# Attention and a top-1 MoE on one core: a new order of the first steps, the roots of two units apart, the gains in two DMAs

## The chip, the core and the metric

The kernel runs on one core of one Trainium2 chip. The metric is the device time of one execution in microseconds. It is taken three times for the kernel before and shown with its median.

## What is computed

Per batch and head, 448 rows of q and k of 64 numbers are normed by their root mean square and multiplied by gains; then comes softmax attention, and a mixture of eight experts follows of which each token takes one.

```
rmsnorm(x, g) = x / sqrt(mean(x*x, -1) + 1e-6) * g
scores = rmsnorm(q, g_q) @ rmsnorm(k, g_k).T / 8        # 8 batches, 12 heads, 448 x 448
attn = exp(scores - max(scores)); attn /= sum(attn) + 1e-9
x = (attn @ v) as 3584 tokens x 768
e = argmax(x @ w_gate + modality_bias[modality_id]); p = softmax of the same at e
out = p * (relu(x @ w1[e]) @ w2[e])                     # 8 experts, 768 -> 1024 -> 768
```

## The kernel before

Attention is cut into 48 units of two heads. A unit takes seven steps of the main loop, one for each 128 of its 896 rows of scores; step n = 7u + j belongs to unit u. Steps from -22 to -1 are a prologue in which only the first units are prepared. The expert part runs behind and beside it; none of it changes here.

Instructions are issued in an order written out by hand, and each engine works through its own list in that order. The table `PLAN` says in which step a piece of a unit is issued. For unit u the pieces are:

- `ld`, the loads of q and k (L833, issued by SP); `lv`, those of v (L826).
- `sq` and `sk`, squares of q and of k. ACT writes them into one buffer for q and one for k (`sq_b`), and a reduction to one sum per row and head follows: one instruction on DVE, or a tree of six on POOL, in place in that buffer, for the pairs (unit, 0 for q or 1 for k) that `ps` lists. The next square of that side has to wait for the reduction.
- `rs`, the roots: two instructions on ACT (Ln, Exp, L53) and five small ones on POOL. Units go in groups of three; `rs0` says from which unit of its group the roots of an entry reach, so that one entry can cover one, two or three units.
- `nq` and `nk`, the norms (x times its root), on POOL; that of q of unit 0 is on DVE.
- `tk` and `tq`, the transposes (`tr{u}_{g}`, g = 0 for q, 1 for k; L908 on PE). ACT then takes the high part out of them and casts it to the places where the scores want it; for k it multiplies by `gs`, the product of both gains. DVE takes the low part, and SP moves some of it (L921).
- `sa`, scores for the row maxima (`sa{u}_{j}`, L985 and L990), each followed by a maximum on DVE.
- `mt`, the transpose of the maxima (L1001). ACT copies it out (7x128), and a DMA lays it into row 64 of the tile `ql` (L1006). That DMA is issued by ACT for the first two and the last three units, by SP for the others.
- `st`, the scores themselves (L1018), two halves: the second one takes the low part and the row of maxima. ACT takes the exponential of each (`st{u}_{j}`), and `av` (L1056, L1060) multiplies by v.
- `warm`, `warm1` and `warm2`: matmuls without use (L1341) that keep PE busy in the prologue. One such call shows as two matmuls in the trace.

`gain_product` makes `gs` on DVE from the gains that `load_gains` fetches. A step's lists are run in a fixed order: PE's work of the step, then what stood over for ACT and DVE, then the exponential, then the maxima, then casts that may wait; squares that a step issues have their reduction at the start of the next step's DVE list.

Of the kernel before, what the change touches and what calls it, by code (L numbers as in the profile page):

```python
# [66 lines left out]
def kernel(  # L67
# [739 lines left out]
    if True:  # L807
# [548 lines left out]
        def at(where, n, fn):  # L1356
            where.setdefault(n, []).append(fn)
# [66 lines left out]
        for n in range(P["start"], NJ * NU):  # L1424
# [22 lines left out]
                sums(*a)  # L1447
            for a in todo.get("gates", ()):
                at(pre["A"], n + 1, gates(*a))
            for a in todo.get("tr", ()):  # L1450
                a0, a1, a2, d_ = tr(*a)
                if a[0] < P["early"]:
                    at(pre["A"], n + 1, a1)
                    at(pre["A"], n + 1, a2)
                    at(pre["A"], n + P["late0"], a0)
                    at(pre["V"], n + P["late0"], d_)
                    continue
                at(pre["A"], n + 1, a0)
# [283 lines left out]
```

## Time and profile before

| | |
|---|---|
| time, median of 3 (lowest to highest) | 1041.18 us (1040.47 to 1041.79) |
| time of the profiled execution | 1043.32 us |
| its span, from the first to the last instruction | 1041.5 us |
| PE, ACT, DVE, POOL busy | 98%, 68%, 71%, 69% |
| mean granted clock of TensorE | 0.996 |

Times in rows are microseconds from the start of the span. Busy shares are means over a prologue in which PE mostly does warm-up work, 48 units of attention, and the experts behind them, so they say little about a stage.

### The profile page before, as it was taken

What the parts mean: (1) busy time and instruction counts of PE and PEld (TensorE: products, weight loads), DVE (VectorE), ACT (ScalarE), POOL (GpSimd) and SP (SyncE); (2) the same over time, 40 slices, a digit from 0 to 9 for tenths busy, and PEclk for the clock granted to TensorE, in tenths of its full rate; (3) what the DMA queues carried; (4) which work ended last, traced back from release to release, by engine and by line L of the source; (5) the groups of instructions that cost most, each with busy time, mean ns of one, the idle gap of its engine ahead of it and who ended that gap; (6) DMA issues with size and microseconds to landing.
All of it is one profiled execution on the core that took longest, in us unless ns stands there. A gap on an engine that the chain in (4) does not pass through costs nothing.

```text
span 1041.5 us, 18863 instructions
## 1 busy us (share of the span) xinstructions
PE 1017.7 (98%) x6462; PEld 820.2 (79%) x6462; DVE 742.2 (71%) x1260; ACT 710.0 (68%) x1379; POOL 718.2 (69%) x747
## 2 busy tenths in 40 slices
PE   8999999999999999999999999999999999999996
PEld 7655666666666666656659999999999999999995
DVE  5777888887888778886667987755675567656740
ACT  6897999889999889887655555645554455545531
POOL 6788798989788887888956646765645555565451
PEclk9999999999999999999999999999999999999998
DMA  6775658868677677665748506234572343234261
GB/s 181 193 172 131 160 139 191 166 143 183 157 170 160 156 177 156 163 119 119 230 120 285 92 17 188 71 92 122 162 263 74 110 122 92 62 92 123 74 201 63
DMA packets 147960, 148.20 MB, mean 142 GB/s; under 512 B 72762, under 2 KB 137742, under 8 KB 147344
## 3 DMA queue, kind: packets, MB, share of 16 engines
q1 hardware_dynamic: 122458, 105.08, 42.7%
q0 software_dynamic: 25328, 41.82, 12.8%
q8 instruction: 53, 0.87, 0.4%
q14 instruction: 51, 0.42, 0.2%
q10 hardware_dynamic: 70, 0.02, 0.0%
HBM read 150.31 MB, written 33.39 MB: 176 GB/s over the span
## 4 chain that ended last, share of the span: by engine, by line
PE 85%; DMA 4%; DVE 3%; ACT 3%; issue 2%; POOL 1%; SPq 1%; ACTq 0%; POOLq 0%; DVEq 0%
PE ph L608 23%; PE py L638 22%; PE st L1018 12%; PE av L1060 10%; PE sa L990 5%; PE av L1056 3%; PE tr L908 3%; PE xt L1126 2%; PE sm L1082 2%; DVE at_hlw L52 1%; PE sm L1089 1%; DMA w1w<-xw 1%; PE mt L1001 1%; DMA xrw<-xg 1%; DMA r<-in_q_dram 1%
## 5 line engine op out<-in xcount | busy, mean ns | idle before, releaser
L608 PE MATMUL ph<-xw,w1w 128*128 128x256 f32 x2016 | 246.3, 283 | 2.1 <-ACT at_w2lw L52 1.3
L608 PEld LDWEIGHTS ph<-xw,w1w 128*128 128x128 f32 x2016 | 243.9, 192 | 3.9 <-ACT at_w2lw L52 1.4
L52 DVE TENSOR_REDUCE at_hlw<-sa 128x1 f32<-128x448 f32 x336 | 205.0, 619 | 30.3 <-PE sa L985 15.2
L1018 PE MATMUL st<-w1w 128*128 128x448 f32 (+1 forms) x480 | 183.4, 431 | 1.5 <-ACT r2w L52 0.9
L52 POOL DMA_INDIRECT r<-in_moe_w_dram,tb_w x60 | 84.6, 1411 | 54.9 <-DVE w1w L52 39.7
L52 ACT ACTIVATE hhw<-ph 128x512 fp32r<-128x512 f32 x56 | 33.5, 598 | 123.4 <-PE ph L608 94.3
L52 ACT ACTIVATE r2w<-st 128x448 f32<-128x448 f32 x168 | 91.1, 545 | 34.6 <-PE st L1018 23.2
L638 PE MATMUL py<-w2lw,hhw 128*128 128x384 f32 x448 | 113.7, 334 | 0.0
L52 DVE TENSOR_TENSOR w1w<-r,w1w 128x768 fp32r<-128x768 f32 x112 | 104.9, 968 | 11.0 <-ACT w1w L52 9.8
L990 PE MATMUL sa<-w1w 128*128 128x448 f32 (+1 forms) x288 | 108.1, 376 | 3.0 <-DVE at_hlw L52 1.2
L52 ACT CAST w1w<-xw 64x448 fp32r<-64x448 f32 x188 | 105.9, 563 | 3.7 <-issue 1.4
L52 POOL DMA_INDIRECT r2w<-in_moe_w_dram,tb_vi x48 | 51.5, 1074 | 81.7 <-DVE w2lw L52 68.1
L52 DVE TENSOR_TENSOR w2lw<-r2w,w2ha 128x1536 fp32r<-128x1536 f32 x28 | 49.1, 1757 | 80.0 <-ACT w2ha L52 49.2
L1018 PEld LDWEIGHTS st<-w1w 128*128 128x128 f32 (+1 forms) x480 | 86.0, 190 | 24.6 <-issue 10.9
L1018 PE MATMUL st<-w1w,w2ha 65*128 65x448 f32 x288 | 100.6, 370 | 0.5 <-DMA w1w<-xw 0.5
L52 ACT ACTIVATE at_w2lw<-st 128x448 f32<-128x448 f32 x168 | 90.6, 545 | 12.5 <-PE st L1018 5.7
L52 POOL TENSOR_TENSOR xrw<-r,at_hlw 112x512 f32<-112x512 f32 x95 | 97.8, 1050 | 0.5
L52 POOL TENSOR_TENSOR r2w<-r2w 128x448 f32<-128x448 f32 (+1 forms) x72 | 83.3, 1157 | 21.3 <-DVE r2w L52 15.0
L52 ACT CAST w1w<-r 128x768 fp32r<-128x768 f32 x112 | 95.2, 903 | 0.1
L52 ACT ACTIVATE yw<-py,ltn 128x384 f32<-128x384 f32 x55 | 29.4, 579 | 77.0 <-PE py L638 48.5
L638 PEld LDWEIGHTS py<-w2lw,hhw 128*128 128x128 f32 x448 | 80.9, 188 | 0.0
L52 POOL TENSOR_TENSOR r2w<-r2w,at_w2lw 64x448 f32<-64x448 f32 (+1 forms) x48 | 55.3, 1151 | 32.8 <-DVE r2w L52 17.4
(302 smaller groups left out, 2210.2 us busy)
## 6 DMA issues: line engine op xcount, KB each, us to landing
w1w<-xw SPq DMA_DIRECT2D x216, 112.0 KB
xg<-xrw SPq DMA_DIRECT2D x14, 768.0 KB
xrw<-xg SPq DMA_DIRECT2D x56, 192.0 KB
r<-in_q_dram SPq DMA_DIRECT2D x19, 448.0 KB
r<-in_k_dram SPq DMA_DIRECT2D x19, 448.0 KB
w2ha<-xw SPq DMA_DIRECT2D x72, 112.0 KB
w1w<-w1w SPq DMA_DIRECT2D x48, 112.0 KB
r2w<-in_v_dram SPq DMA_DIRECT2D x24, 224.0 KB
```

What stands on the lines that cost most here:

```text
L52: return fn(*a, **kw)
L608: PE.matmul(ps[:, i], lhsT=lt_, rhs=rt_[:, c], start=n == 0, stop=n == 17)
L638: PE.matmul(ps[n][:, :384], lhsT=lt_[:, j, 128 * t : 128 * t + 128], rhs=rt_[:, 384 * n : 384 * n + 384], start=j == 0 and m == 0, stop=j ...
L908: PE.transpose(sp[:, c], src[:, c], idn[:CP, :CP])
L990: PE.matmul(ps[:, :S], lhsT=t["qq"][r, h, a : a + 128], rhs=t["kk"][h][r], start=True, stop=True)
L1001: PE.transpose(ps[0:NJ, :128], t["mx"], idn)
L1018: PE.matmul(ps[:, :S], lhsT=l, rhs=t["qq"][:, h] if first else t["ql"][0:65, h], start=first and (j != 3 or h == 0), stop=not first and (j ...
L1056: PE.matmul(t["av"][:, :S], lhsT=vd_b[u % 2], rhs=t["p"][:, 3], start=False, stop=True)
L1060: PE.matmul(t["av"][64 * h : 64 * h + 64, :S], lhsT=vv[:, u % 3, j], rhs=t["p"][:, j], start=c == 0, stop=False)
L1082: PE.matmul(R[g][32 * i : 32 * i + 32, :S], lhsT=sel[:, m], rhs=T[u + i // 2]["cs"][:, i % 2], start=m == 0, stop=False, tile_position=(0, ...
L1089: PE.matmul(sm[32 * i : 32 * i + 32, :S], lhsT=wg[:, (4 * g + i) % NP], rhs=T[4 * g + i]["xt"], start=False, stop=True, tile_position=(0, ...
L1126: PE.transpose(ps[:CP, 128 * c : 128 * c + 128], T[u]["xt"][:, c * CP : (c + 1) * CP], idn)
```

## The change

Entries of `PLAN` (step before, step after), the rest as it was:

```
nk1 -16 -> -17    nq1 -13 -> -16    nq2 -8 -> -13     norms of units 1, 2
sk4 -15 -> -10
sq5 -15 -> -6     sq4  -8 -> -7     sk8 5 -> 8   sq8 5 -> 10     squares
rs1 none -> -18   rs2 -16 -> -15 (units 1 and 2 -> unit 2)   rs5 -7 -> -5     roots
tk3 0 -> 2        nk5 0 -> 2        ld7, ld8: two entries more, at -7 and 2
warm at -13: 5 -> 1    warm2 at -13: 5 -> 1 (the entry goes, the default stands)
ps [(6,1),(4,0),(3,0),(2,0)] -> [(6,1),(3,0)]     lv of unit 0: -10 -> -7
```

So the roots of units 1 and 2, made together before, are made one unit after the other; the reductions of q of units 2 and 4 go from POOL to DVE; squares of units 4, 5 and 8 are issued at other places; the transpose of k of unit 3 comes two steps later; and eight warm-up calls fewer run on PE. The code around it:

```diff
-            for half in range(2):
-                SY.dma_start(gg[64 * half : 64 * half + 64, 0:1], g_q.unsqueeze(1))
-                SY.dma_start(gg[64 * half : 64 * half + 64, 1:2], g_k.unsqueeze(1))
+            for i, g in enumerate((g_q, g_k)):
+                SY.dma_start(gg[:, i : i + 1], bass.AP(tensor=g.tensor, offset=g.offset, ap=[[0, 2], [1, 64], [1, 1]]))
...
-                (A if u < 2 or u >= NU - 3 else SY).dma_start(t["ql"][64:65].rearrange("p h s -> p (h s)").bitcast(F32),
+                (A if u == 1 or u >= NU - 3 else SY).dma_start(t["ql"][64:65].rearrange("p h s -> p (h s)").bitcast(F32),
...
+            if ("mt", 0) in plan.get(n, ()):
+                at(pre["A"], n + 1, mt(0))
             for a in todo.get("tr", ()):
...
             for a in todo.get("mt", ()):
-                at(pre["A"], n + 1, mt(*a))
+                if a[0]:
+                    at(pre["A"], n + 1, mt(*a))
...
+                if a == (0, 0):
+                    gain_product()
                 norm(*a, V if a in P["nv"] else G)
-                if a == (0, 1):
-                    gain_product()
```

The gains take two DMAs in place of four; the source of each reads the 64 numbers twice, for 128 partitions. The row of maxima of unit 0 is issued by SP. The transpose of its maxima comes ahead of the transpose of k of unit 2 (`tr2_1`) in the same step. The product of the gains stands directly ahead of the norm of q of unit 0.

What this moves on the engines shows in their lists. First DVE at the start (`xrw` <- `r` is the norm of q of unit 0; reductions go from `xrw`, the buffers of squares, to `at_hlw`). Before:

```order
L52 TENSOR_REDUCE at_hlw_169<-xrw_160 112x8 x2
L52 TENSOR_TENSOR gs_91<-gg_90 128x1
L52 TENSOR_SCALAR gs_91<-gs_91 128x1
L52 TENSOR_REDUCE at_hlw_169<-xrw_160 112x8 x2
L52 MEMSET w2ha_164 65x3x64
L52 MEMSET w1w_161 65x64
L52 TENSOR_TENSOR xrw_160<-r1_0_158,at_hlw_169 112x2x4x64
L52 SCALAR_TENSOR_TENSOR xw_162<-tr0_1_244,gs_91,xw_162 128x448
```

And with the change:

```order
L52 TENSOR_REDUCE at_hlw_169<-xrw_160 112x8 x4
L52 TENSOR_TENSOR gs_91<-gg_90 128x1
L52 TENSOR_SCALAR gs_91<-gs_91 128x1
L52 MEMSET w2ha_164 65x3x64
L52 MEMSET w1w_161 65x64
L52 TENSOR_TENSOR xrw_160<-r1_0_158,at_hlw_169 112x2x4x64
L52 SCALAR_TENSOR_TENSOR xw_162<-tr0_1_240,gs_91,xw_162 128x448
L52 TENSOR_REDUCE at_hlw_169<-xrw_160 112x8 x2
```

The two reductions of unit 1 (the second "x2" of before) now stand ahead of the product of the gains, and those of unit 2 follow behind `tr0_1`.

Second, DVE around the end of unit 0's maxima and the start of unit 1's (`sa0_`, `sa1_` are scores; a reduction from `xrw` is one of squares). Before:

```order
L52 TENSOR_REDUCE at_hlw_169<-sa0_6_364 128x1
L52 TENSOR_REDUCE at_hlw_169<-sa0_3_376 128x1
L52 TENSOR_REDUCE at_hlw_169<-xrw_160 112x8
L52 SCALAR_TENSOR_TENSOR xw_162<-tr2_1_386,gs_91,xw_162 128x448
L52 TENSOR_REDUCE at_hlw_169<-sa1_0_423 128x1
L52 TENSOR_REDUCE at_hlw_169<-sa1_1_430 128x1
```

And with the change:

```order
L52 TENSOR_REDUCE at_hlw_169<-sa0_6_353 128x1
L52 TENSOR_REDUCE at_hlw_169<-xrw_160 112x8
L52 TENSOR_REDUCE at_hlw_169<-sa0_3_365 128x1
L52 TENSOR_REDUCE at_hlw_169<-xrw_160 112x8
L52 SCALAR_TENSOR_TENSOR xw_162<-tr2_1_376,gs_91,xw_162 128x448
L52 TENSOR_REDUCE at_hlw_169<-xrw_160 112x8 x2
L52 TENSOR_REDUCE at_hlw_169<-sa1_0_405 128x1
L52 TENSOR_REDUCE at_hlw_169<-sa1_1_412 128x1
```

Where one reduction of squares stood between the last maximum of unit 0 and the first of unit 1, there are three now, and one more stands ahead of the last maximum of unit 0: those of k of units 4 and 5 and of q of units 4 and 5.

Third, ACT between the last exponentials of unit 0 and the first of unit 1 (`xrw` <- `r1_1` is a square of k, `r1_0` of q). Before:

```order
L52 ACTIVATE r2w_163<-st0_5_539 128x448
L52 ACTIVATE xrw_160<-r1_1_159 112x512
L52 ACTIVATE xrw_160<-r1_0_158 112x512
L52 CAST xw_162<-tr3_0_544 128x448
L52 ACTIVATE r2w_163<-st0_6_554 128x448
L52 CAST w1w_161<-xw_162 64x448
L52 CAST w2ha_164<-xw_162 64x64
L52 ACTIVATE xrw_160<-r1_1_159 112x512
```

And with the change, from the square of k of unit 6 on:

```order
L52 ACTIVATE xrw_160<-r1_1_159 112x512
L52 CAST w1w_161<-xw_162 64x448
L52 CAST w2ha_164<-xw_162 64x64
L52 ACTIVATE at_w2lw_167<-st1_0_560 128x448
L52 ACTIVATE at_w2lw_167<-st1_1_577 128x448
L52 ACTIVATE xrw_160<-r1_1_159 112x512
L52 ACTIVATE xw_162<-tr4_1_585,gs_91 128x448
L52 CAST xw_162<-mt2_590 7x128
```

The squares of unit 8 (the two rows behind `st0_5` of before) have moved behind the first exponentials of unit 1: that of k stands behind `st1_1` and ahead of `tr4_1`, that of q, not shown, behind `st1_3`. Ahead of the square of k of unit 8 the one of k of unit 6 is now the last to use that buffer; its reduction is the one that POOL does (6, 1).

## Rows read from the trace of the kernel before

**Rows 1.** Page, busy time of each engine over the span.

```profile
PE 1017.7 (98%) x6462; PEld 820.2 (79%) x6462; DVE 742.2 (71%) x1260; ACT 710.0 (68%) x1379; POOL 718.2 (69%) x747
```

**Rows 2.** Windows: length, then busy us and instructions of each engine, PEclk, DMA.

```profile
40.00:50.00 10.00, 9.20 (x46) 5.79 (x46) 7.97 (x14) 9.54 (x23) 7.98 (x12) 1.00 0.68 161
80.00:100.00 20.00, 18.71 (x96) 11.47 (x95) 15.66 (x29) 15.47 (x35) 16.19 (x19) 1.00 0.62 141
100.00:120.00 20.00, 20.00 (x109) 12.81 (x108) 17.01 (x31) 17.95 (x42) 16.59 (x20) 1.00 0.58 138
```

**Rows 3.** Timeline of DVE: start, us, instruction, idle before and its releaser.

```profile
4.62 1.42 DVE L52 TENSOR_REDUCE at_hlw<-xrw 112x8 f32<-112x512 f32 x2 [2.17 <-ACT xrw L52]
9.61 0.16 DVE L52 TENSOR_TENSOR gs<-gg 128x1 f32<-128x1 f32 x1 [3.57 <-DMA gg<-in_g_k_dram]
9.88 1.27 DVE L52 TENSOR_REDUCE at_hlw<-xrw 112x8 f32<-112x512 f32 x2
11.35 0.62 DVE L52 TENSOR_TENSOR xrw<-r,at_hlw 112x512 f32<-112x512 f32 x1
```

**Rows 4.** Timeline of ACT, first squares and the shared roots.

```profile
7.55 1.15 ACT L52 ACTIVATE xrw<-r 112x512 f32<-112x512 f32 x2 [0.83 <-DMA r<-in_k_dram]
15.24 0.68 ACT L53 ACTIVATE at_hlw<-at_hlw,lnb 112x32 f32<-112x32 f32 x2
```

**Rows 5.** DMA view, 7.5 to 8 us, then 56 to 57 us.

```profile
DMA packets 144, 0.02 MB, mean 42 GB/s; under 512 B 124, under 2 KB 144, under 8 KB 144
q1 hardware_dynamic: 144, 0.02, 30.6%
...
DMA packets 1488, 0.08 MB, mean 81 GB/s; under 512 B 1488, under 2 KB 1488, under 8 KB 1488
q1 hardware_dynamic: 1488, 0.08, 92.2%
```

**Rows 6.** Timeline of POOL, one reduction and the three norms.

```profile
11.89 2.27 POOL L52 TENSOR_TENSOR xrw<-xrw 112x256 f32<-112x256 f32 x5 [2.84 <-ACT xrw L52]
17.29 3.05 POOL L52 TENSOR_TENSOR xrw<-r,at_hlw 112x512 f32<-112x512 f32 x3
```

**Rows 7.** Timeline of PE, unit 0 from its second score to its maxima.

```profile
16.70 1.60 PE L1341 MATMUL warm<-idn,ones 128*128 128x128 f32 x12
19.85 0.55 PE L908 MATMUL tr<-idn,xrw 112*128 112x112 f32 x4
25.09 0.28 PE L1001 MATMUL mt<-idn,at_hlw 128*7 128x128 f32 x1 [0.20 <-DVE at_hlw L52]
30.48 0.44 PE L1018 MATMUL st<-w1w,w2ha 65*128 65x448 f32 x1 [0.49 <-DMA w1w<-xw]
```

**Rows 8.** Timeline of DVE, first maxima of unit 1.

```profile
27.17 1.81 DVE L52 TENSOR_REDUCE at_hlw<-sa 128x1 f32<-128x448 f32 x3 [0.31 <-PE sa L990]
```

**Rows 9.** Timeline of ACT, 26 to 44 us.

```profile
26.32 1.32 ACTq L52 DMA_DIRECT2D w1w<-xw  x1
27.68 0.56 ACT L52 CAST w1w<-xw 64x448 fp32r<-64x448 f32 x1 [1.39 <-issue]
...
38.30 1.15 ACT L52 ACTIVATE xrw<-r 112x512 f32<-112x512 f32 x2
...
41.16 0.63 ACT L52 ACTIVATE xrw<-r 112x512 f32<-112x512 f32 x1 [0.25 <-DVE at_hlw L52]
...
42.55 0.98 ACT L52 ACTIVATE at_w2lw<-st 128x448 f32<-128x448 f32 x2
43.55 0.64 ACT L52 ACTIVATE xw<-tr,gs 128x448 fp32r<-128x448 f32 x1
```

**Rows 10.** Timeline of POOL, reduction of k of unit 6.

```profile
41.87 2.55 POOL L52 TENSOR_TENSOR xrw<-xrw 112x256 f32<-112x256 f32 x5 [1.39 <-ACT xrw L52]
44.49 0.20 POOL L52 TENSOR_TENSOR at_hlw<-xrw 112x8 f32<-112x8 f32 x1
```

**Rows 11.** Windows of 1 us: busy of each engine, then PEclk.

```profile
10.00:11.00 1.00, 0.00 (x0) 0.00 (x0) 1.00 (x2) 0.41 (x1) 0.00 (x0) 1.00 0.86 256
12.00:13.00 1.00, 0.97 (x5) 0.98 (x6) 0.00 (x0) 0.97 (x3) 0.92 (x2) 0.50 0.80 275
```

More of the change, by code (lines that the diff above doesn't have):

```diff
@@ L33 @@
 ET = mybir.EngineType
-PLAN = {'rtj': 6, 'rushat': 36, 'av': (1, 1, 4, 6), 'xt': 4, 'xte': (2, 5), 'sm': 4, 'la': 4, 'rc': 9, 'csv': (1,), 'csj': (3, 6), 'csd': (1, 1), 'cse': (2, 1), 'sa': 14, 'mt': 6, 'tk': 21, 'tq': 18, 'nq': 26, 'nk': 26, 'sk': 49, 'sq': 50, 'rs': 48, 'ld': 58, 'first': {('sq', 0): -22, ('sk', 0): -21, ('nk', 0): -20, ('nq', 0): -18, ('sq', 1): -19, ('sk', 1): -19, ('sq', 2): -18, ('sk', 2): -18, ('nk', 1): -16, ('nq', 1): -13, ('tk', 0): -18, ('tq', 0): -17, ('sa', 0): -15, ('tk', 1): -13, ('tq', 1): -11, ('sa', 1): -5, ('mt', 0): -8, ('tk', 2): -8, ('tq', 2): -3, ('nq', 2): -8, ('nk', 2): -14, ('nq', 3): 3, ('nk', 3): -3, ('sq', 3): -13, ('sk', 3): -13, ('sq', 4): -8, ('sk', 4): -15, ('sq', 6): -2, ('sk', 6): 6, ('sk', 7): 11, ('sq', 8): 5, ('sk', 8): 5, ('nk', 7): 20, ('nq', 9): 31, ('tq', 3): 5, ('mt', 1): 2, ('nq', 5): 6, ('mt', 8): 50, ('rs', 0): -20, ('rs', 2): -16, ('nq', 8): 35, ('rs', 5): -7, ('mt', 2): 8, ('nq', 7): 25, ('mt', 5): 30, ('sk', 9): 15, ('tk', 9): 42, ('mt', 6): 37, ('nq', 6): 17, ('sa', 5): 23, ('rs', 8): 16, ('mt', 4): 23, ('nk', 4): -2, ('ld', 9): 6, ('tk', 5): 16, ('sk', 5): -9, ('tk', 3): 0, ('tk', 4): 8, ('nk', 5): 0, ('sq', 5): -15, ('mt', 3): 16, ('nq', 4): 1, ('sa', 4): 16, ('tq', 4): 12, ('sa', 3): 9, ('sa', 2): 1, ('tq', 5): 19, ('mt', 7): 44, ('tq', 7): 31, ('sa', 7): 37, ('nk', 6): 16, ('tq', 6): 24, ('sq', 7): 12, ('tk', 6): 21, ('sa', 6): 30, ('tk', 7): 28}, 'rs0': {0: 0, 2: 1, 5: 0, 8: 0}, 'sastep': 1, 'start': -22, 'warm': {-22: 15, -21: 3, -20: 1, -16: 4, -15: 1, -13: 5, -10: 2, -7: 3, -6: 1, -5: 1, 5: 1, 7: 1}, 'warmn': 1, 'early': 1, 'late0': 1, 'pmp0': 2, 'ramp': 10, 'pmp': (0, 0, 1, 1, 1, 0, 1), 'nv': [(0, 0)], 'pmpa': (1, 0, 1, 0, 1, 1, 1), 'rush': (1, 1, 1), 'ps': [(6, 1), (4, 0), (3, 0), (2, 0)], 'pa': [], 'rtr': 6, 'sml': 4, 'lv': (-10, 0), 'lg': 16, 'lz': 13, 'gc': 43, 's1': (1, 4), 'vcopy': 8, 'warm1': {0: 4, 1: 2, 2: 1}, 'warm2': {-13: 5}, 'xs': 7, 'gc2': 64}
@@ new lines @@
+PLAN = {'rtj': 6, 'rushat': 36, 'av': (1, 1, 4, 6), 'xt': 4, 'xte': (2, 5), 'sm': 4, 'la': 4, 'rc': 9, 'csv': (1,), 'csj': (3, 6), 'csd': (1, 1), 'cse': (2, 1), 'sa': 14, 'mt': 6, 'tk': 21, 'tq': 18, 'nq': 26, 'nk': 26, 'sk': 49, 'sq': 50, 'rs': 48, 'ld': 58, 'first': {('sq', 0): -22, ('sk', 0): -21, ('nk', 0): -20, ('nq', 0): -18, ('sq', 1): -19, ('sk', 1): -19, ('sq', 2): -18, ('sk', 2): -18, ('nk', 1): -17, ('nq', 1): -16, ('tk', 0): -18, ('tq', 0): -17, ('sa', 0): -15, ('tk', 1): -13, ('tq', 1): -11, ('sa', 1): -5, ('mt', 0): -8, ('tk', 2): -8, ('tq', 2): -3, ('nq', 2): -13, ('nk', 2): -14, ('nq', 3): 3, ('nk', 3): -3, ('sq', 3): -13, ('sk', 3): -13, ('sq', 4): -7, ('sk', 4): -10, ('sq', 6): -2, ('sk', 6): 6, ('sk', 7): 11, ('sq', 8): 10, ('sk', 8): 8, ('nk', 7): 20, ('nq', 9): 31, ('tq', 3): 5, ('mt', 1): 2, ('nq', 5): 6, ('mt', 8): 50, ('rs', 0): -20, ('rs', 2): -15, ('nq', 8): 35, ('rs', 5): -5, ('mt', 2): 8, ('nq', 7): 25, ('mt', 5): 30, ('sk', 9): 15, ('tk', 9): 42, ('mt', 6): 37, ('nq', 6): 17, ('sa', 5): 23, ('rs', 8): 16, ('mt', 4): 23, ('nk', 4): -2, ('ld', 9): 6, ('tk', 5): 16, ('sk', 5): -9, ('tk', 3): 2, ('tk', 4): 8, ('nk', 5): 2, ('sq', 5): -6, ('mt', 3): 16, ('nq', 4): 1, ('sa', 4): 16, ('tq', 4): 12, ('sa', 3): 9, ('sa', 2): 1, ('tq', 5): 19, ('mt', 7): 44, ('tq', 7): 31, ('sa', 7): 37, ('nk', 6): 16, ('tq', 6): 24, ('sq', 7): 12, ('tk', 6): 21, ('sa', 6): 30, ('tk', 7): 28, ('ld', 8): 2, ('ld', 7): -7, ('rs', 1): -18}, 'rs0': {0: 0, 2: 2, 5: 0, 8: 0, 1: 1}, 'sastep': 1, 'start': -22, 'warm': {-22: 15, -21: 3, -20: 1, -16: 4, -15: 1, -13: 1, -10: 2, -7: 3, -6: 1, -5: 1, 5: 1, 7: 1}, 'warmn': 1, 'early': 1, 'late0': 1, 'pmp0': 2, 'ramp': 10, 'pmp': (0, 0, 1, 1, 1, 0, 1), 'nv': [(0, 0)], 'pmpa': (1, 0, 1, 0, 1, 1, 1), 'rush': (1, 1, 1), 'ps': [(6, 1), (3, 0)], 'pa': [], 'rtr': 6, 'sml': 4, 'lv': (-7, 0), 'lg': 16, 'lz': 13, 'gc': 43, 's1': (1, 4), 'vcopy': 8, 'warm1': {0: 4, 1: 2, 2: 1}, 'warm2': {}, 'xs': 7, 'gc2': 64}
```

## The prediction

> **What bounds the kernel now.** I read three views in this order. The busy shares come first: PE is busy 98% of the span [rows 1], so a gain can only come from what PE waits for, or from work without use that is taken off it, and the change edits almost only the prologue, where that work stands. Second, the windows say how far a shift made there is carried. From 40 to 50 us ACT is the fullest engine, 9.54 of 10 us; from 80 to 100 us PE has 18.71 of 20; from 100 us on it has 20.00 of 20 [rows 2]. From there everything hangs on PE, so what counts is by how much PE's work at 100 us comes earlier or later. No load holds that stretch, so I carry a shift of ACT at 44 us over in full and keep the 1.3 us that PE idles between 80 and 100 us as a possible cushion. Third, the timelines of the first 44 us, one engine after the other, give the steps below. There the chain is: first squares, roots and norms; transposes; maxima of unit 0; maxima of unit 1; then ACT, with casts, exponentials and squares almost without a gap.
>
> The steps are differences inside one execution, which took 1043.32 us for a span of 1041.5; that is 2.14 us above the median of the three runs, 1041.18. I add the sum of the steps to the median.
>
> **The change, part by part.**
>
> *Start.* DVE has its first two reductions done at 6.04 and then idles 3.57 us for the gains, until 9.61. Two reductions of 1.27 us stand behind the product of the gains, and the norm of q of unit 0 starts at 11.35 [rows 3]. The squares of unit 1 that they read end at 8.70 [rows 4]; the reductions last some 0.60 each beyond the overlap, so in front of the product they end at about 9.4. They go into the idle time, and the norm starts at 11.35 - 1.27 = 10.08: 1.27 us earlier, if the gains land when they did.
>
> *Gains.* Two DMAs save two issues of SP, which nobody waits for: the gains are queued behind the loads of q and k. Whether they land earlier or later the trace can't say directly, as no DMA of this form is in it. They consist of 256 packets of 4 bytes now and afterwards, over 16 engines now. From below: with two issues fewer they land at most 0.2 us earlier in effect, because the reductions hold DVE until 9.4 anyway. From above: small packets cost between 16 x 0.922 / 1488 us = 9.9 ns (a stretch of nothing but small packets) and 16 x 0.5 x 0.306 / 144 us = 17 ns of an engine (the stretch in which the gains run) [rows 5]. If all 256 fell to two engines, each would have 128 in place of 16, and 112 x 9.9 to 17 ns = 1.1 to 1.9 us more would pass, if those two were also the last to reach them. They need not be: the slowest of 16 sets the landing now. I take +0.2 us, and keep -0.2 and +1.9. The Trainium skill (DMA: Bandwidth & Descriptors, sections "Why a DMA increments its semaphore by 16 and not by 1" and "Rules for kernel authors") says that the outermost dimension of size two, which repeats the source, confines each of these DMAs to two engines. By that rule alone the sum would be 1.1 to 1.9 us above the one without this term; no run shown here has such a DMA.
>
> *Roots of unit 1 apart.* Before, the shared roots wait for POOL's reduction of q of unit 2, five instructions from 11.89 to 14.16 and a sixth [rows 6]; they run at 15.24 [rows 4], and the three norms at 17.29 [rows 6]. With the change they wait only for unit 1's reductions, which end at 9.4; but they stand behind both squares of unit 2 on ACT (1.15), so they run at about 10.1 to 10.8. POOL took 1.37 us from the end of the shared ones (15.92) to 17.29, so the norms of unit 1 run from about 12.2, five us earlier. They no longer hold `tr1_1`; PE's own list does. There eight warm-up calls are gone, 0.27 us each (six, shown as 12 matmuls, took 1.60) [rows 7]: 2.1 us. With the 1.1 us of the start (1.27 less the wait for two new roots of 0.2 on ACT) `tr1_1` comes 3.2 to 3.6 us earlier than its 19.85 [rows 7]; I take 3.4.
>
> *Maxima of unit 0 and 1.* One more reduction (0.60) stands on DVE ahead of the last maximum of unit 0. Its transpose, at 25.09 [rows 7], comes 3.4 - 0.6 = 2.8 us earlier, at 22.3. Then the lead is lost. The squares of q of units 4 and 5 now stand on ACT between the casts of `tr2_1`; they share a buffer, so it goes: cast of the maxima (0.24), high part (0.64), cast (0.56), square (0.6), its reduction (0.65), square (0.6), reduction (0.65), with some 0.3 of hand-overs, and only then the first maximum of unit 1: 22.3 + 4.3 = 26.6, against 27.17 [rows 8]. What is left is 0.6 us of the 2.8.
>
> *Row of maxima by SP.* ACT loses the issue of 1.32 us, shown as a gap of 1.39 before the next cast [rows 9]. SP issues it at about 23; even with the 4.2 us from issue on ACT to the second half of `st0_0` (26.32 to 30.48, of which 0.49 was a wait for it [rows 7]) it lands at 27.2, before `st0_0` needs it. With the 0.6 from above and this wait gone, `st0_0` leads by about 1.2 us. That is not 0.6 plus 1.39, since the maxima, not ACT, set unit 1's next steps.
>
> *Squares of unit 8.* ACT gives up 1.15 us of squares at 38.30 [rows 9]. Part of that is hidden, and the late transpose of k of unit 3 puts its two casts (1.13) behind `st0_3`; the square of k of unit 6, which ended at 41.79 [rows 9], I put at 40.4, a lead of 1.4. So the exponentials of `st1_0` and `st1_1`, over at 43.53 [rows 9], end at 42.0. Next on ACT is now the square of k of unit 8. It overwrites the buffer in which POOL adds up k of unit 6: five instructions of 2.55 and one of 0.20, which began 0.08 behind that square [rows 10]. POOL is done at 40.4 + 0.1 + 2.75 = 43.2. ACT stands still for 1.2 us, then squares for 0.57, and the high part of `tr4_1`, at 43.55 [rows 9], starts at 43.8: 0.25 later. Behind it queue the maxima of unit 2 and the exponentials of unit 1, for which PE waits. The square of q adds 0.57 two exponentials on: +0.8 us.
>
> *At nothing:* loads and v moved behind others (needed far later), and `gs` one place earlier on DVE. If loads came late, `sq` of unit 7 would show it first.
>
> Sum: +0.8 for ACT at 48 us, +0.2 for the gains, which delay the norm and all behind it: +1.0, or 1042.2 us. Bounds: the lead at `st0_0` kept and no wait for POOL gives -1.2; the cushion eating all of it 0; gains at their worst +2.7.
>
> **Rivals.** *The lead is kept (faster).* The chain of squares between units 0 and 1 may overlap better than I drew it, DVE having its reductions done before the scores are there. Then 2.8 us stay at `st0_0`; the wait for POOL shrinks none of that, since it is a wait relative to the square of unit 6, but 2.8 - 1.2 + 1.4 of issue time given back holds about 2.5 to 3.0: 1038.2 to 1038.7. For it speaks that ACT is nearly full and loses 1.4 us of issue; against it the single buffer.
>
> *Gains late (slower).* The mechanism is above: 128 packets on each of two engines, and `gs` at 11.5 instead of 9.61. All of the start shifts by 1.9: 1041.18 + 0.8 + 1.9 = 1043.9. It decides for slower from a landing 1.3 us late on. Against it: the norm has 1.27 us of lead to lose first, which this counts already.
>
> *The clock (slower).* PE stands still from 10 to 11 us, and at 12 to 13 the granted clock is 0.50 [rows 11]. With eight warm-up calls gone it may stay or fall there again. PE has some 4 us of real work between `tr1_1` and the maxima's transpose; by the warm-up calls, 0.13 us a matmul at 1.00 [rows 7], doubled at half clock, up to 3 us more: 1044.9. It decides from 1.1 us on. Against it: scores and transposes themselves fill that stretch, closer together than before.
>
> *It reaches nothing.* The shifts end in the cushion before 100 us: 1041.2.
>
> **How the numbers follow.** Forecast 0.50; lead kept 0.23; gains late 0.11; clock 0.08; nothing 0.08. A measurement of this kernel tells about 0.2% (2.1 us) from no change. The forecast is inside that, as is the last case: 0.58 the same. Faster 0.23, slower 0.19. Within the forecast alone I expect 1040.5 to 1043.2. The range leaves out half of the faster case and the worst of the two slower ones, about 0.2: 1038.6 to 1044.0.
>
> **What would show it.** In the new trace: the norm of q of unit 0 on DVE near 10.1 with gains as its releaser no later than 9.9; `tr1_1` near 16.4; the transpose of unit 0's maxima near 22.3; the first maximum of unit 1 near 26.6 with a square of ACT just before; no DMA issue of ACT at 26; a square on ACT near 43 that waits about 1.2 us for POOL. I am wrong if `st0_0` leads by over 2 us, if that square does not wait, if `gs` starts after 11, or if a granted clock of 0.5 stands between 16 and 22 us.

## The result and the profile after

| | before | with the change |
|---|---|---|
| median of 6 runs (lowest to highest) | 1040.99 us (1038.05 to 1042.40) | 1048.62 us (1046.34 to 1050.45) |
| ratio, 95% interval | | 1.008 (1.0063 to 1.0097) |
| span of the profiled execution | 1041.5 us | 1044.5 us |
| mean granted clock of TensorE there | 0.996 | 0.990 |

The kernel is slower by 0.8%, 7.6 us of medians; 1042.2 us had been forecast, no measurable change. The profiled execution is the fastest of its six, so its span holds only 3.0 us of the loss. In all six the mean clock is below the 0.996 of the profile of before: 0.986 to 0.993.

The start of DVE, in the timeline after (answers to [rows 3]):

```profile
8.11 1.28 DVE L52 TENSOR_REDUCE at_hlw<-xrw 112x8 f32<-112x512 f32 x2 [2.13 <-ACT xrw L52]
9.30 0.15 DVE L52 TENSOR_TENSOR gs<-gg 128x1 f32<-128x1 f32 x1
9.84 0.62 DVE L52 TENSOR_TENSOR xrw<-r,at_hlw 112x512 f32<-112x512 f32 x1
```

The product of the gains has no wait in front of it: they had landed by 9.30, and the norm starts 1.5 us earlier than before. PE and its clock after (answers to [rows 7] and [rows 11]):

```profile
15.42 0.47 PE L989 MATMUL sa<-w1w 64*128 64x448 f32 x1 [0.62 <-DVE at_hlw L52]
16.15 0.55 PE L907 MATMUL tr<-idn,xrw 112*128 112x112 f32 x4
23.29 0.38 PE L1000 MATMUL mt<-idn,at_hlw 128*7 128x128 f32 x1
28.90 0.47 PE L989 MATMUL sa<-w1w 128*128 128x448 f32 x1 [0.59 <-DVE at_hlw L52]
46.85 0.47 PE L1017 MATMUL st<-w1w 128*128 128x448 f32 x1 [0.93 <-ACT at_w2lw L52]
```

```profile
15.00:16.00 1.00, 0.58 (x2) 0.36 (x3) 0.97 (x3) 1.00 (x3) 0.65 (x3) 1.00 0.86 194
16.00:17.00 1.00, 1.00 (x7) 0.66 (x7) 0.55 (x1) 0.36 (x2) 0.90 (x2) 1.00 0.75 172
18.00:19.00 1.00, 1.00 (x4) 0.64 (x4) 1.00 (x3) 0.54 (x1) 1.00 (x2) 0.50 0.64 207
26.00:27.00 1.00, 1.00 (x6) 1.00 (x6) 0.69 (x1) 0.81 (x3) 0.00 (x0) 0.50 0.59 138
...
370.00:371.00 1.00, 0.32 (x2) 0.32 (x3) 0.66 (x2) 0.35 (x1) 1.00 (x2) 1.00 0.85 149
373.00:374.00 1.00, 1.00 (x6) 0.33 (x4) 1.00 (x2) 0.61 (x2) 1.00 (x2) 0.50 0.92 253
```

`tr1_1` comes at 16.15, 3.7 us earlier. But PE now stands still before it, for 0.62 us, and from 17.1 to 27.4 us (by the clock's own records) PE has half its clock, 1.2 GHz in place of 2.4. A matmul of scores takes 0.74 us there in place of 0.47, and the transpose of the maxima comes at 23.29. A second such stretch stands at 372.1 to 375.5, behind another wait of PE. Before had one in the prologue, at 11.9 to 15.3, and none later but at the end.

ACT and POOL after (answers to [rows 9, 10]):

```profile
36.30 1.31 ACTq L52 DMA_DIRECT2D w1w<-xw  x1
37.66 0.54 ACT L52 ACTIVATE r2w<-st 128x448 f32<-128x448 f32 x1 [1.39 <-PE sa L984]
...
43.14 0.98 ACT L52 ACTIVATE at_w2lw<-st 128x448 f32<-128x448 f32 x2
45.07 0.63 ACT L52 ACTIVATE xrw<-r 112x512 f32<-112x512 f32 x1 [0.95 <-POOL at_hlw L52]
45.60 0.61 ACT L52 ACTIVATE xw<-tr,gs 128x448 fp32r<-128x448 f32 x1
```

```profile
42.46 2.29 POOL L52 TENSOR_TENSOR xrw<-xrw 112x256 f32<-112x256 f32 x5 [0.41 <-ACT xrw L52]
44.83 0.20 POOL L52 TENSOR_TENSOR at_hlw<-xrw 112x8 f32<-112x8 f32 x1
```

The square of k of unit 8 waits 0.95 us for POOL, as the prediction drew it. The row of unit 0 has left ACT, but the row of unit 1 now pays 1.31 us and a gap of 1.39 for its issue; before it had paid 0.76:

```profile
35.61 0.76 ACTq L52 DMA_DIRECT2D w1w<-xw  x1
```

In the table below "lag" is by how much later than in the profile of before the transpose of a unit's maxima on PE starts (before: unit 1 at 35.02, 2 at 43.67, 3 at 54.43, 32 at 360.28, 33 at 369.90, 34 at 381.84). "Half clock" leaves out the stretch at the end that every kernel has. The medians of before differ, as the chips of the batches do; each ratio is to before on the same chip.

| kernel | lag at 1, 2, 3 | lag at 32, 33, 34 | half clock, us | median, median of before | ratio (95%) | mean clock of runs |
|---|---|---|---|---|---|---|
| the change | 0.3, 0.3, 2.4 | 1.9, 5.3, 4.0 | 17.1-27.4, 372.1-375.5 | 1048.62, 1040.99 | 1.008 (1.0063-1.0097) | 0.989 |
| the same again | 0.4, 0.5, 3.6 | 3.3, 7.1, 5.7 | 28.4-31.9, 48.9-52.3, 373.2-376.6, 543.9-550.7 | 1047.31, 1041.42 | 1.006 (1.0039-1.0081) | 0.991 |
| warm-ups back | -0.3, -0.2, 4.2 | 4.7, 4.8, 3.9 | 47.6-54.4 | 1044.94, 1041.42 | 1.0035 (1.0012-1.0057) | 0.994 |
| unit 8's squares back | -0.3, 1.4, 1.4 | 1.2, 5.3, 4.0 | 27.5-30.9, 372.2-375.6 | 1045.53, 1041.42 | 1.0037 (1.0016-1.0057) | 0.994 |
| both back | 1.1, 2.8, 2.8 | 2.6, 2.6, 2.5 | 29.7-33.2 | 1045.37, 1041.42 | 1.0033 (1.0007-1.0059) | 0.995 |
| warm-ups back, k of unit 6 by DVE | -0.6, -0.6, 0.5 | 2.8, 2.8, 3.1 | none | 1043.65, 1042.71 | 0.9998 (0.9973-1.0023) | 0.996 |
| squares of units 4, 5 back | 3.1, 3.2, 6.0 | 5.8, 8.0, 6.6 | 14.9-25.1, 35.4-38.8, 52.4-55.9 | 1049.00, 1042.71 | 1.0051 (1.0027-1.0074) | 0.990 |
| first part only | -1.5, -1.0, -1.0 | -1.0, -1.0, -1.0 | none | 1041.87, 1042.71 | 0.9988 (0.9962-1.0013) | 0.996 |
| before, fewer warm-ups | -1.7, -1.7, -1.7 | 2.9, 4.7, 3.2 | 11.7-15.1, 243.8-247.2, 540.8-544.2 | 1047.15, 1042.71 | 1.003 (1.0000-1.0061) | 0.992 |
| the change, short calls | 2.2, 2.3, 6.6 | 7.2, 7.5, 7.4 | 15.9-26.2, 50.1-56.9 | 1050.07, 1045.37 | 1.0028 (1.0005-1.0052) | 0.991 |
| before, short calls | 4.7, 4.6, 4.6 | 5.2, 5.2, 5.4 | 11.8-15.2, 18.6-32.3, 544.3-551.1 | 1050.76, 1045.37 | 1.0035 (1.0001-1.0070) | 0.989 |
| first part and loads | -0.8, 0.0, 0.0 | 0.1, 0.2, 0.0 | none | 1044.09, 1045.37 | 1.0005 (0.9983-1.0027) | 0.995 |
| first part, long calls | -2.1, -1.6, -1.6 | -0.6, 3.3, 1.9 | 369.4-372.8, 533.3-536.7 | 1047.70, 1045.37 | 1.0014 (0.9992-1.0036) | 0.994 |

### The profile page after: what moved, and what is told of

It is laid out like the page before. It is cut to its first block, busy times and chain, and to the rows that moved or that the text cites. A ratio compares the mean times of both kernels' runs of the same rounds, so it can differ in the third digit from the quotient of the medians.

```text
span 1044.5 us, 18825 instructions
## 1 busy us (share of the span) xinstructions
PE 1019.4 (98%) x6446; PEld 821.9 (79%) x6446; DVE 744.0 (71%) x1262; ACT 710.4 (68%) x1381; POOL 708.3 (68%) x740
## 4 chain that ended last, share of the span: by engine, by line
PE 88%; DVE 5%; ACT 2%; DMA 2%; issue 2%; POOL 1%; SPq 1%; ACTq 0%; POOLq 0%; DVEq 0%
PE ph L607 22%; PE py L637 21%; PE st L1017 13%; PE av L1059 11%; PE sa L989 5%; PE tr L907 3%; PE av L1055 3%; PE xt L1125 2%; DVE at_hlw L52 2%; PE sm L1081 2%; PE warm L1340 1%; PE sm L1088 1%; PE mt L1000 1%; PE sa L984 1%; DMA xrw<-xg 1%
## 5 line engine op out<-in xcount | busy, mean ns | idle before, releaser
L52 DVE TENSOR_REDUCE at_hlw<-sa 128x1 f32<-128x448 f32 x336 | 204.7, 618 | 31.5 <-PE sa L984 15.3
L52 ACT ACTIVATE r2w<-st 128x448 f32<-128x448 f32 x168 | 91.0, 545 | 34.8 <-PE st L1017 27.4
L52 POOL TENSOR_TENSOR r2w<-r2w 128x448 f32<-128x448 f32 (+1 forms) x72 | 82.9, 1152 | 25.1 <-DVE r2w L52 18.0
```

Source lines behind the costliest of these rows:

```text
L52: return fn(*a, **kw)
```

## The experiments

The theories were: 1, the clock falls behind gaps that the missing warm-up calls leave; 2, the wait of ACT for POOL loses what the prologue gained; 3, the loss arises behind the prologue. Two more came up on the way: 4, the lead of unit 0 is lost by the chain of squares ahead of unit 1's maxima; 5, the count of PE's instructions decides where later fetches of instructions fall.

**Warm-up calls back.**

```diff
-'warm': {... -13: 1, ...}, 'warm2': {}
+'warm': {... -13: 5, ...}, 'warm2': {-13: 5}
```

> The change with its eight warm-up calls put back at step -13. Theory 1, the clock: the half clock that the profile of the change shows from about 17 to 27 us is owed to the two gaps of PE before it; with the calls back it stays at 1.00 there, and the transpose of the maxima of unit 1 comes at about 34 us in place of 35.3, some 1.5 us earlier; the end comes 1.5 us earlier or more. Theory 2, the wait of the square of k of unit 8 for POOL: nothing of the 2.0 us between the transposes of maxima of units 2 and 3 changes. Theory 3, the loss arises behind the prologue: the time stays within 1 us of the change's.

No half clock came before 47.6 us, and unit 1 is 0.6 us earlier than in the change, less than the 1.5 expected. The wait of ACT for POOL is the same 0.95 us, and behind it PE's waits of 0.90 and 0.59 us were followed by a half clock; so this profile lags 4.2 us at unit 3 and yet its median is below the change's. The ratio fell from 1.006 to 1.0035, 2.4 us of medians on the same chip, though the two intervals overlap; theory 3 does not give that for an edit before 20 us by itself.

**Squares of unit 8 back.**

```diff
-('sq', 8): 10, ('sk', 8): 8
+('sq', 8): 5, ('sk', 8): 5
```

> The change with both squares of unit 8 back at step 5. Theory 2: the wait of ACT for POOL at 44 us is gone, the lag of PE against before does not grow by 2.0 us between the transposes of maxima of units 2 and 3, and the end comes about 2 us earlier than that of the change. Theory 1: the half clock at 17 to 27 us stays, and with it a lag of about 0.3 us at unit 2. Theory 3: the time stays within 1 us of the change's.

The wait for POOL is gone and the lag stands still from unit 2 to 3, but 1.7 us arise between units 1 and 2, where they did not in before with the squares at the same place. There the two casts of `tr3_1` stand behind the exponential `st0_3` now, and the costly issue of the row stands just ahead; that these two are the cause is read from ACT's list, and no run puts `tk3` back alone. So the gain over the change is 1.0 us at unit 3, half of what theory 2 gave. The half clock of 17 to 27 us, which theory 1 expected to stay, did not come; one came at 27.5.

**Both back.** Both edits above in one kernel.

> Both edits together. Theories 1 and 2 together make the prologue 1 to 1.5 us faster than before, with a time of about 1039.5 to 1040.5; if only one of them holds, it lies 2 us higher. Theory 3: 1047 to 1049, as the change.

A miss: 1045.37, five us above what theories 1 and 2 gave together. A half clock at 29.7 to 33.2 us, behind a wait of PE of 2.06 us ahead of unit 1's third score, holds part of it: from unit 1's first maximum to the transpose of its maxima pass 8.5 us here and in the two other profiles with a half clock in this place (the change again, unit 8's squares back), 7.1 us in the change and the two with warm-ups back, where it is full. The 1.7 us between units 1 and 2 stand here as in the run before. More than these two edits is wrong, and the gains do not add.

**The change again.**

> The change as it is, for a second profile, since its runs spread over 4 us. Theories 1 and 2: the same half clock before 30 us and the same wait of ACT for POOL at 44 us; a lag of PE of 2.4 us at 54 us. Theory 3: what differs between the runs is behind 100 us, as the half clock at 372 us of the first profile.

The half clock of 17 to 27 us did not come back, and the lag at 54 us is 3.6 in place of 2.4. The lag at unit 1 is nearly the same, 0.4 us, though the first half clock comes at 28.4 here. Two things came back: the wait behind POOL (followed by a half clock this time) and the one at unit 33, with its half clock at 373 us. A mean clock of 0.9914 in these runs against 0.9956 in those of before is, over 1046 us, 2 x 0.0042 x 1046 = 8.8 us more at half clock; where PE has work all the time each costs a half, 4.4 of the 5.9 us between the medians (an estimate, and for the half clock wherever it fell).

**Warm-up calls back and k of unit 6 by DVE.**

```diff
-'ps': [(6, 1), (3, 0)]
+'ps': [(3, 0)]
```

> The change with its eight warm-up calls back and with the squares of k of unit 6 added up by DVE instead of POOL, which frees their buffer some 2 us earlier. Theory 1, the clock, with what set it off: in the run with the calls alone the gaps of PE at 46 to 48 us, behind the wait of ACT for POOL, were followed by a half clock at 47.6 us. Without that wait no half clock follows there, the lag of PE at 54 us falls from 4.2 to about 0.5 us, and the time is 2 us or more below that run, about 1042. Rival, the calls alone make the difference and the wait of ACT is hidden: the lag stays within 1 us of the run with the calls alone where its clock was full, about 2 us, and the time within 1 us of it.

As theory 1 said: the lag at unit 3 is 0.5, and the time is that of before, within an interval of 0.9973 to 1.0023. Beyond what it said, no half clock appears at all ahead of the one at the end. PE's wait of 2.06 us at 28 us, which in the kernel with both back comes ahead of a half clock, stands here too and none follows it. In the timeline of ACT the square of k of unit 8 follows the exponentials without a wait:

```profile
42.22 0.98 ACT L52 ACTIVATE at_w2lw<-st 128x448 f32<-128x448 f32 x2
43.22 0.64 ACT L52 ACTIVATE xrw<-r 112x512 f32<-112x512 f32 x1
43.76 0.62 ACT L52 ACTIVATE xw<-tr,gs 128x448 fp32r<-128x448 f32 x1
```

**Squares of units 4 and 5 back.**

```diff
-('sq', 4): -7, ('sk', 4): -10, ('sq', 5): -6     'ps': [(6, 1), (3, 0)]
+('sq', 4): -8, ('sk', 4): -15, ('sq', 5): -15    'ps': [(6, 1), (4, 0), (3, 0)]
```

> The change with the squares of units 4 and 5 back at their steps, and that of q of unit 4 added up by POOL again. Theory 4, the lead is lost by the chain of squares and reductions ahead of unit 1's first maxima: the gap of PE of 2.05 us at 27 us is gone, the transpose of unit 1's maxima comes 2 us earlier or more than in the change, at about 33 us, and no half clock follows at 27 to 31 us; the end comes some 3 us earlier than the change's. Rival, the lead is lost on ACT by its casts (the transpose of k of unit 3 two steps later) and by the first DMA that ACT issues: the first maximum of unit 1 comes earlier, but the transpose of unit 1's maxima at 35 us or later, and the time stays as the change's.

The time is a miss: 1.0051 against 1.006 of the change again, not 3 us less. Of theory 4 the first part holds: the gap at 27 us is gone, and from the transpose of unit 0's maxima to the first maximum of unit 1 pass 2.9 us in place of 4.5. The rest cannot be read here: a half clock from 14.9 to 25.1 us covers the stretch, and a move that comes late makes PE wait 2.34 us at 35.35, so that unit 1's maxima are transposed at 38.1, as late as the rival had it.

**First part only.** The change with squares, `tk3`, `nk5`, `rs5`, loads and warm-up calls as before.

```diff
-sq4 -7, sk4 -10, sq5 -6, sq8 10, sk8 8, tk3 2, nk5 2, rs5 -5, ld8 2, ld7 -7, lv 0 -7, warm -13: 1, warm2 none, ps (6,1) (3,0)
+sq4 -8, sk4 -15, sq5 -15, sq8 5, sk8 5, tk3 0, nk5 0, rs5 -7, no ld7 and ld8, lv 0 -10, warm -13: 5, warm2 -13: 5, ps (6,1) (4,0) (3,0)
```

> Only the first part of the change: roots of units 1 and 2 apart, the gains in two DMAs, the row of maxima and the transpose of unit 0's maxima; all squares of units 4, 5 and 8, the transpose of k of unit 3, the loads and the warm-up calls as before. By theory 1 and 4 together: no new gap of PE over 1 us, the granted clock as before, and a lag of -1 to 0 us at 54 us; the time within 1.5 us of before. Rival, the first part itself makes gaps on PE, since it brings work earlier than its successors: half clock before 35 us and a time 2 us or more above before.

As theories 1 and 4 said, but for one gap of PE over 1 us: it waits 1.41 us at 29.12 for the row of maxima, which SP issues at 25.57, behind three loads. The lead is 1.5 us at unit 1 and 1.0 from unit 2 to the end, and the clock is that of before. The first maxima on DVE, of the change again and then of this kernel, show theory 4:

```profile
26.95 1.80 DVE L52 TENSOR_REDUCE at_hlw<-sa 128x1 f32<-128x448 f32 x3
```

```profile
24.87 1.81 DVE L52 TENSOR_REDUCE at_hlw<-sa 128x1 f32<-128x448 f32 x3 [0.43 <-PE sa L989]
```

The transposes of unit 0's maxima are alike (22.46 and 22.38), so it is the squares, casts and reductions between them that take 2.1 us. The same stretch takes 4.5 us in all five profiles with the squares moved and a full clock there, with the calls or without, and 2.5 us in all three kernels with the first part only. The ratio, 0.9988, does not tell this kernel from before.

**Before with fewer warm-ups.**

```diff
-'warm': {... -13: 5, ...}, 'warm2': {-13: 5}
+'warm': {... -13: 1, ...}, 'warm2': {}
```

> The kernel before without eight of its warm-up calls, as the change has it. Theory 1: PE then idles about 2 us at 17 to 20 us, where it waits for the norms of unit 1; a half clock follows, and the time is 1 to 3 us above before. Rival: the calls only fill idle time and nothing depends on them: the time stays within 1 us of before, and the clock is 1.00 from 16 us on.

The time came out as theory 1 said (1.003, from 1.0000 to 1.0061), in another way. PE waits only 0.16 us for the norms; the prologue is 1.7 us faster, with the clock of before, and the clock is full from 15.1 us on, as the rival had it, until 243.8. But the lag rises by 4.6 us between units 3 and 32, then by 1.8 at unit 33, and there are half clocks at 244 and 541 us. An edit at 17 us that works at 240 and 370 us was what theory 3 had asked for, and it led to theory 5.

The jump at unit 33 stands in all five profiles of kernels with eight calls fewer so far (by the table 3.4, 3.8, 4.1, 2.2 and 1.8 us) and in none of the other five. What happens there is seen in the change. SP's timeline first, then the DMA view from 365 to 368 us, then PE:

```profile
363.00 1.00 SPq L1005 DMA_DIRECT2D w1w<-xw  x1
364.09 4.50 SPq L920 DMA_DIRECT2D w1w<-xw  x4
```

```profile
365.39 2.56 SPq L920 DMA_DIRECT2D w1w<-xw  x1
```

```profile
q1 hardware_dynamic: 153, 0.22, 32.0%
q8 instruction: 1, 0.02, 5.1%
```

```profile
368.67 0.36 PE L1017 MATMUL st<-w1w,w2ha 65*128 65x448 f32 x1
370.68 0.44 PE L989 MATMUL sa<-w1w 128*128 128x448 f32 x1 [1.65 <-DVE at_hlw L52]
```

One of four moves takes SP 2.56 us to issue in place of 0.55, while one 16 KB packet of an instruction queue (q8) is under way; a score for unit 33's maxima waits 1.65 us, and the half clock of 372 us follows. The row names a maximum on DVE, but DVE had done its last maximum by 368.54; in the four other profiles the wait in this place, 1.50 to 2.03 us, is put down to the move itself. In before a packet of that queue falls there too, but earlier in the program: it begins 0.9 us ahead of the transpose of unit 32's maxima, in the change 2.9 us behind it. So the stalled issue is one of two moves that nobody waits for, and the four moves go out unhindered:

```profile
359.35 2.59 SPq L921 DMA_DIRECT2D w2ha<-xw  x2
362.94 2.44 SPq L921 DMA_DIRECT2D w1w<-xw  x4
```

The Trainium skill (Runtime: NRT & Kernel Launch, section "Instruction fetch mechanics") says that an engine's instruction memory is refilled by DMA in blocks of 16 KiB. The 53 packets of q8 on the profile's page agree: 0.87 MB, 16.4 KB each. The section calls the cost of crossing the border of such a block mostly hidden; for an issue of SP beside the fetch these traces show otherwise, and what the engine that is fed pays no run shows.

**The change with short calls.** Eight calls of 8 columns at the places of the eight that are gone.

```diff
+        def short(n):
+            for _ in range(n):
+                PE.matmul(wps[:, :8], lhsT=ones, rhs=idn[:, :8], start=True, stop=True)
...
+            if n == -13:
+                short(4)
```

> The change with eight useless calls of 8 columns in place of the eight warm-up calls that it took away: as many instructions on PE as in the runs with the calls back, but hardly any work. Theory 5: the 16 KB fetches of the instruction queue come at points that the count of PE's instructions sets; one of them stalls an issue of SP for over 2 us at about 365 us where the calls are missing, a move for unit 33 is late, PE waits and its clock halves. Then the lag does not jump by 2 to 4 us at unit 33 here, while the gaps and the half clock before 50 us stay as in the change; time about 1045 to 1046. Theory 1 alone (only the clock in the prologue and what follows it): the jump at unit 33 is there again, time 1047 to 1049.

The jump at unit 33 is gone (0.3), as theory 5 said. On this batch's chip before itself takes 1045.37, so the time is read by its ratio: 1.0028 (1.0005 to 1.0052), where theory 5's 1045 to 1046 are 1.003 to 1.005 of the before of the earlier batches and theory 1's 1047 to 1049 are 1.005 to 1.008; it lies nearer to theory 5. The prologue of the profile is worse than expected: a lag of 6.6 us at unit 3, with half clocks at 15.9 to 26.2 and, behind the wait for POOL, at 50.1 to 56.9.

**Before with short calls.** The same lines in the kernel before without the eight calls.

> The kernel before without the eight warm-up calls, but with eight of 8 columns in their place. Its sister without any of them led by 1.7 us at 54 us and lost 3.8 us behind 230 us. Theory 5: with the instructions back the lead of about 1.7 us is kept, there is no jump at unit 33, and the time is 1 to 2 us below before. Rival: the eight calls matter by the work that they put on PE; then the time stays some 4 us above before, as without them.

Again no jump at unit 33, but in the time the rival came true: 1.0035 (1.0001 to 1.0070), by the ratio 3.7 us above before. In the profile PE stands at half clock from 18.6 to 32.3 us, behind which it lags 4.6 us, and at 544 us. Its sister without any calls had kept the full clock there, so one profile of each does not show what the calls do to the clock. The means of all runs do: 0.9906 and 0.9891 with short calls against 0.9947 of before in the same batch, and 0.9915 without any against 0.9952.

**First part and loads.** First part only, with `ld7`, `ld8` and `lv` as in the change.

> The first part of the change alone, as in the run that led by 1.0 us at 54 us, but with the loads of units 7 and 8 and of v of unit 0 at the steps that the change gives them, behind the row of maxima on SP's queue. There PE waited 1.41 us at 29 us for that row. Theory: the row is issued 1.5 us earlier, PE's wait goes, and the lag at 54 us is about -2; time about 1 us below that run and 1.5 us or more below before. Rival: another move or the exponentials are late next, and the lag stays at -1.

A miss. The row is issued at 23.53 in place of 25.57, and the wait for it at 29 us is gone, but a move is late next (PE waits 1.39 us at 32.92), and the lag is 0.0 in place of -2.

**First part with long calls.** First part only, the same columns of warm-up work in eight calls fewer.

```diff
+        def long(n):
+            PE.matmul(wps[:, : 128 * n], lhsT=ones, rhs=idn.unsqueeze(1).to_broadcast([128, n, 128]), start=True, stop=True)
...
+            if n == -13:
+                long(4)
+            if n == -16:
+                long(2)
+                long(2)
```

> The first part of the change alone with the same warm-up work on PE, but in eight calls fewer: eight calls of 128 columns are merged into two of 512, and four into two of 256. Theory 5: the lag at 54 us is about -1 as with single calls, but the fetch of PE's instructions falls at about 363 to 366 us, a jump of 2 to 4 us follows at unit 33, and the time is some 2 us or more above the run with single calls, at 1044 or more. Rival: the work of the calls is what counts; then the time stays within 1 us of that run, at about 1042.

As theory 5 said, and with a full clock in the prologue: a lead of 1.6 us at unit 3, 0.6 at unit 32, turns into a lag of 3.3 at unit 33. The DMA view from 362 to 365 us, SP, PE and its windows:

```profile
q8 instruction: 1, 0.02, 5.3%
```

```profile
361.15 0.79 SPq L1005 DMA_DIRECT2D w1w<-xw  x1
362.04 4.47 SPq L920 DMA_DIRECT2D w1w<-xw  x4
```

```profile
368.60 0.44 PE L989 MATMUL sa<-w1w 128*128 128x448 f32 x1 [2.07 <-DMA w1w<-xw]
```

```profile
368.00:369.00 1.00, 0.40 (x3) 0.39 (x4) 0.13 (x1) 0.00 (x0) 1.00 (x3) 1.00 0.70 117
370.00:371.00 1.00, 1.00 (x4) 0.30 (x4) 0.86 (x2) 0.95 (x3) 0.92 (x2) 0.50 0.29 91
```

With single calls the same four moves took 2.44 us, at 361.93, and PE did not wait. Counting all, the jump stands in six of six profiles with the small count of instructions and in none of eight with the other, that of before included; the packet begins 2.6 to 2.9 us behind the transpose of unit 32's maxima in the six and 0.5 to 1.0 us ahead of it in the eight. Where a half clock follows, the jump is 3.4 to 4.1 us, and in the two profiles without one 1.8 and 2.2. In the time the step from single to long calls does not stand clear of the noise: 1.0014 (0.9992 to 1.0036) against 0.9988 (0.9962 to 1.0013).

The mean clock of the runs with long calls is 0.9944, that of before in this batch 0.9947. So the calls matter twice: the clock of all runs goes with what they do on PE, the jump at unit 33 with their count.

## Why the prediction was wrong

- *Start and gains.* The norm was put at 10.08, 0.2 later by the gains; it came at 9.84. Two engines or not, the gains were there by 9.30, so the rival of late gains is out. Which engines they used no run shows.
- *Roots apart.* `tr1_1` was put at 16.4 and came at 16.15. The transpose of unit 0's maxima was put at 22.3; it came at 23.29 with the half clock, and at 22.46 and 21.72 in two profiles of that list whose clock was full until then. Right.
- *Lead lost before unit 1's first maxima.* Put at 26.6; it came at 28.23 behind the half clock, and at 26.95 and 26.22 in those two. From the transpose ahead of it 4.3 us were given, and 4.5 pass where the clock is full; the first part alone has 2.5. Shown, and about the size given.
- *Row of maxima by SP.* Mis-sized. It was to free ACT of a gap of 1.39 us. That cost belongs to the first DMA that ACT issues, not to the row of unit 0: the issue is 1.32 us for the first and 0.76 for the second in before, and 1.31 for the first one after. So 0.76 us left the list, and the costly one now stands at 36 us among the exponentials.
- *Squares of unit 8 and POOL.* A wait of 1.2 us and a loss of 2.0 (from a lead of 1.2 to a lag of 0.8) were given (43.53 less the lead of 1.4 is 42.1 and not 42.0, so 1.1 by its own rows); the wait is 0.95, and the lag grows by 2.0 between units 2 and 3 where the clock stays full. Right in place and size, but the level was wrong: unit 1 had no lead left to lose. In the four other profiles of kernels with this wait a half clock followed it 3.1 to 4.5 us later, and the lag grew by 2.8 to 4.4. Without the wait (k of unit 6 by DVE) it still grew by 1.1, so not all of this is the wait.
- *The step that failed: the eight warm-up calls, taken as a gain of "2.1 us" with nothing lost.* Their removal was to be harmless unless the clock fell, a rival with 0.08. Taking them out of before alone gives 1.003 (1.0000 to 1.0061), and putting them back into the change brings it from 1.006 to 1.0035. It leaves gaps of PE in which the clock falls (17 to 27 us here, the very sign that the prediction named; at other places in other runs). At unit 1 that is 0.6 us, a lag of 0.3 against a lead of 0.3 with the calls back. The rest of the forecast lead of 1.2 did not come with the calls either: there `st0_0` leads by 0.2 us, and by 0.5 with k of unit 6 on DVE. And it moves the later fetches of instructions, which costs a jump of 1.8 to 4.1 us at unit 33, of which 1.3 to 1.5 is won back by unit 34. No row of the prediction reached beyond 120 us, where I carried the sum unchanged.
- *Size.* With the calls back and POOL's reduction on DVE no loss is left that the runs can tell (0.9998, 0.9973 to 1.0023). That the loss lies in these two alone is not shown: with the calls back and the squares of unit 8 at their old steps, so without the wait as well, the ratio is 1.0033 (1.0007 to 1.0059). How the 7.6 us of medians divide between clock, wait and fetch is not settled: the half clock stretches differ from run to run, and of a kernel's runs in a batch only one has a trace. The lags that arise at 234 to 255 us in some profiles (in before with fewer warm-ups PE waits 2.37 us there for a move) and the half clocks at 533 to 550 us were not taken apart.

## What to carry to other kernels

Filler work on PE is part of the schedule: take it out only where the wait that it covers has gone too, and compare the granted clock of all runs, not of the profiled one alone. A wait of under 1 us on an engine that PE hangs on can cost more than its length by the clock behind it. An edit at the start of a long unrolled program also changes how many instructions stand in front of everything that follows; where a loss shows far behind the edit, keep the count and change the work, and the other way round.

## What had not been expected of the hardware

- While a 16 KB packet of the instruction queue q8 is under way, an issue of a DMA on SP can take 1.5 to 3.5 us in place of 0.55 (before: 1.96 us at 226.7, 1.63 at 341.3, 2.03 at 359.9, with packets beginning at 225.9, 341.1 and 359.3). It need not: 34 issues of before that stand beside such a packet took no longer than 1.2 us, and a few long ones have none beside them. Where those packets fall goes with the count of PE's instructions.
- The first DMA that ACT issues takes 1.31 or 1.32 us on its queue, the later ones 0.73 to 0.77, in all fourteen traces.
- Behind waits of PE of 0.39 and 0.62 us at 12.9 and 15.4 us the clock fell to 0.50 at 17.1; in a second profile of the same kernel, behind the same two waits, it stayed at 1.00 until 28.4.
